# Sixteen weight loads moved from SyncE's queue to GpSimd's

## The chip, the cores and the metric

The kernel runs on one core of one Trainium2 chip. The metric is the device time of one execution in microseconds (us). The core has five engines that run their own instruction queues side by side: TensorE (PE; its weight loads are shown as PEld), VectorE (DVE), ScalarE (ACT), GpSimd (POOL) and SyncE (SP). Transfers between main memory and the on-chip memory are carried out by 16 DMA engines. An instruction on some engine's queue issues the transfer; a semaphore tells when it has landed.

## The reference

Two blocks follow each other. The first is a gated linear recurrence over 768 tokens (S) for 4 batches (B) and 8 heads (H) with head size 48 (D), with complex gates. The second is a two-layer MLP on the 3,072 resulting rows of 384 numbers, with a leaky rectifier that has one slope per feature:

```python
mag = np.sqrt(a_re * a_re + a_im * a_im)
scale = np.minimum(mag, 0.999) / (mag + 1e-06)
a_re_n, a_im_n = (a_re * scale, a_im * scale)
for t in range(S):
    new_re = ar * S_re - ai * S_im          # ar, ai: the gates of token t
    new_im = ar * S_im + ai * S_re
    S_re, S_im = (new_re + kv, new_im)      # kv: outer product of k[t] and v[t]
    y[:, :, t] = np.einsum('bhd,bhde->bhe', q[:, :, t], S_re)

x = y.transpose(0, 2, 1, 3).reshape(B * S, H * D)   # 3072 x 384
h = x @ w_in                                         # w_in: 384 x 2048
g = np.maximum(h, 0.0) + alpha * np.minimum(h, 0.0)
return (g @ w_out).astype(np.float32)                # w_out: 2048 x 384
```

The two weight matrices arrive as 64-bit floating point numbers. The kernel loads them as raw 32-bit words and makes 32-bit floats of them on the chip.

## The kernel before, in words

The 3,072 tokens are cut into 24 units of 128 tokens, six for each batch, and each unit holds all eight heads. The recurrence is not stepped through token by token. Inside a unit it is solved by doubling over block lengths 1, 2, 4, 8, 16 and 32 (the tile KQ is multiplied on DVE by decays T at line 638, and PE forms products at line 597), and a state St is carried from one half unit to the next.

**Gates.** The function `gates` turns a_re and a_im of 1, 2 or 3 units at a time into decays and phases. It loads both into the tile gate (line 264). For the last units of a batch a memset on GpSimd (line 263) clears the last column first. DVE begins with line 272, which needs a_re; line 284 is the first that needs a_im. The phases are stored to main memory as phs (line 325), the decays as decs (line 362), after a small memset on GpSimd (line 352). Each unit reads its part back as PP (line 508) and T (two loads, line 515). DVE's first work on a unit (line 580) needs PP, its first doubling step (line 638, reading WQ and T) needs T.

**Other loads of a unit.** KQ takes four loads (lines 500 and 502). In the last unit of a batch GpSimd clears the tail of KQ (line 495). V takes three small loads, VL takes ten of 24 or 48 KB (line 548) and two from a scratch copy of v called vsc (line 552; vsc is written at line 481). The result of a unit goes out as ysc (line 779) and comes back, turned, as xT (lines 795 and 800), the input of the MLP.

**Weights.** The function `pieces` loads both matrices raw, in eight parts each, in the order in0, out0, in1, out1 ... in7, out7. Each part is 768 KB: 128 partitions with three rows of 2,048 bytes for w_in or two of 3,072 for w_out. There are four regions, used in turn, so a load has to wait until ACT has read the part that was loaded four before it. The function `to_f32` turns a part into 32-bit floats in five instructions: three on ACT, which read the raw words (lines 436, 438, 440; after the last one the region is free), and two on DVE (lines 444 and 446). Only then can PE use the weights, at lines 820, 842, 870 and 960.

**Masks.** At the start GpSimd builds four masks out of memsets, affine selects (lines 173 and 175) and copies (line 183). DVE uses them at line 621.

**The order.** Nothing reorders the instructions while the kernel runs. Each function above is a task that stops at every `yield`. A string of letters written out by hand (`ORDER`, lines 30 to 70) says which task goes on next, each letter running one task up to its next `yield`. So the string fixes the order of instructions in each engine's queue. An engine executes its queue strictly in order, and an instruction that waits holds back all behind it. Before the change every load and store of the kernel is issued by SP, in one hardware queue. GpSimd has only the masks and some memsets.

Of the kernel before, what the change touches and what calls it, by code (L numbers as in the profile page):

```python
# [98 lines left out]
def kernel(  # L99
# [32 lines left out]
    nc = tc.nc  # L132
# [248 lines left out]
    def region(name, f):  # L381
        i = (2 * f + (name == "out")) % 4
        at = 18 * MT + i * 4 * DM
        return R[f"raw{i}"], shared[:, at:at + 4 * DM]
# [8 lines left out]
    def pieces():  # L393

        t = yield DMA(8)
        with nc.allow_non_contiguous_dma(reason="one token"):
            nc.sync.dma_start(start[0:D2:2], kv_in[:, :, :, 0].rearrange("b d h -> d b h"))
        done["start", 0] = t
        t = yield DMA(8)
        nc.sync.dma_start(al_1, alpha)  # L400
        t = yield DVE(NF, t)
        nc.vector.tensor_scalar(out=al_1, in0=al_1, scalar1=-1.0, scalar2=1.0, op0=ALU.mult, op1=ALU.add)
        done["alpha", 0] = t

        if words:
            wi = w_in.bitcast(U32).rearrange("(c p) (f e two) -> f p c e two", p=P, e=2 * P, two=2)
            wo = w_out.bitcast(U32).rearrange("(f r p) (e two) -> f p r e two", p=P, r=2, two=2)
        else:
            wi = w_in.rearrange("(c p) (f e) -> f p c e", p=P, e=2 * P)
            wo = w_out.rearrange("(f r p) e -> f p r e", p=P, r=2)  # L410
        for f in range(NF // 2):
            for name, src in (("in", wi), ("out", wo)):
                t = yield DMA(788 if words else 394, takes=(region(name, f)[0],))
                raw = region(name, f)[1]
                if words:
                    raw = raw.bitcast(U32).rearrange("p (c e two) -> p c e two", c=src[f].shape[1], two=2)
                else:
                    raw = raw[:, 0:NK * 2 * P].rearrange("p (c e) -> p c e", c=src[f].shape[1])
                raws[name, f] = raw
                nc.sync.dma_start(raw, src[f])  # L420
                done["raw", name, f] = t

    def to_f32(dst, *key):
# [671 lines left out]
    with tc.manual_schedule():  # L1095
        for i, g in enumerate(GATES):
            plan.add(gates(i, *g))
        plan.add(loads())
        plan.add(half_rows())
        plan.add(loads_v())  # L1100
        plan.add(pieces())
        plan.add(weights("in"))
        plan.add(weights("out"))
        for u in range(NU):
            plan.add(unit(u))
        plan.add(loads_x())
        plan.add(all_mlp())
        plan.run(ORDER)
# [37 lines left out]
```

## Time and profile before

| | |
|---|---|
| median of 3 runs | 773.71 us (771.02 to 776.0) |
| profiled execution | 772.89 us |
| its span in the profile | 771.2 us, 26,837 instructions |
| PE busy | 680.0 us (88%) |
| DVE busy | 606.4 us (79%) |
| ACT busy | 491.8 us (64%) |
| POOL busy | 12.3 us (2%), 48 instructions |
| DMA | 130.61 MB, mean 169 GB/s; hardware queue q1 128.91 MB |
| the sixteen weight loads (line 420) on SP | 8 with a median of 607 ns, 8 with 462 ns; from 8.3 to 155.5 us |

The profile divides the span into 40 equal slices and gives each engine's busy share of a slice in tenths, 9 being 90% or more. The row DMA is the mean busy share of the 16 DMA engines. A timeline line gives the start in us, the duration in us, the engine, the line of the kernel, the operation, the tile written and the tile read, shapes and the count. A bracket at its end tells how long the engine sat idle before it, and what ended the idle time. SPq is SP's queue of transfer issues: the duration is that of the issue, not of the transfer. A windows line gives, for a stretch of the span, the busy us of PE, PEld, DVE, ACT and POOL with instruction counts, then the granted TensorE clock, the DMA share (which can pass 1 where packets overlap) and GB/s.

### The profile page before, as it was taken

To read this page: it belongs to the slowest core of one execution; us is meant where nothing else is said; L and a number is where in the kernel's file an instruction comes from. 1 tells how busy PE (TensorE), PEld (TensorE's weight loads), DVE (VectorE), ACT (ScalarE), POOL (GpSimd) and SP (SyncE) were. 2 spreads that over 40 slices of the span, in tenths; PEclk is the share of its full clock that TensorE was granted. 3 is DMA by queue.
4 is the path that set the end of the run, shared out by engine and by line. 5 is a ranking of instruction groups with operands and counts; after the bars stand their busy time and mean duration, and the time that the engine had idled before them with its cause. 6 is when DMAs were issued, how large, how long until landed. Compare 5 with 4: busy or idle time off the path is not lost.

```text
span 771.2 us, 26837 instructions
## 1 busy us (share of the span) xinstructions
PE 680.0 (88%) x11728; PEld 585.2 (76%) x11728; DVE 606.4 (79%) x798; ACT 491.8 (64%) x933; POOL 12.3 (2%) x48
## 2 busy tenths in 40 slices
PE   0024687899999999999999999999999999999998
PEld 0013565667776888888888888888988888889987
DVE  7888879999999699898998699889977747652323
ACT  7967787896557667857775756856676454453330
POOL 5000000000000000000000000000000000000000
PEclk9999578999999999999999999999999999999999
DMA  9979899679677687686568745794556535411000
GB/s 246 274 216 262 241 286 267 179 228 281 147 168 193 189 199 198 185 236 143 148 164 225 192 99 141 203 277 96 153 141 191 135 88 122 124 38 58 1 21 20
DMA packets 177180, 130.61 MB, mean 169 GB/s; under 512 B 66280, under 2 KB 168424, under 8 KB 176616
## 3 DMA queue, kind: packets, MB, share of 16 engines
q1 hardware_dynamic: 177064, 128.91, 63.1%
q8 instruction: 92, 1.51, 0.8%
q14 instruction: 24, 0.20, 0.1%
HBM read 100.52 MB, written 35.42 MB: 176 GB/s over the span
## 4 chain that ended last, share of the span: by engine, by line
PE 55%; DVE 12%; DMA 8%; ACT 7%; SPq 6%; issue 3%; DVEq 0%; ACTq 0%
PE ps_h L842 17%; PE ps_o L960 15%; PE ps_h L820 4%; PE ps_lv L597 4%; DVE KQ L638 4%; PE ps_y L761 4%; PE ps_o L870 3%; DMA T<-decs 3%; PE ps_kv L721 3%; PE ps_y L747 3%; SPq L548 2%; DMA PP<-phs 2%; PE ps_kt L709 1%; PE ps_h L960 1%; DVE WQ L580 1%
## 5 line engine op out<-in xcount | busy, mean ns | idle before, releaser
L842 PE MATMUL ps_h<-xT,w_in_sb 128*128 128x256 f32 x960 | 228.6, 384 | 0.4 <-DVE shared L857 0.2
L842 PEld LDWEIGHTS ps_h<-xT,w_in_sb 128*128 128x128 f32 x960 | 176.5, 190 | 22.9 <-DVE shared L857 0.9
L638 DVE TENSOR_TENSOR KQ<-KQ,T 96x1024 f32<-96x1024 f32 x120 | 145.8, 1216 | 24.2 <-PE ps_lv L597 12.1
L857 DVE TENSOR_TENSOR shared<-shared,ps_h 128x512 f32<-128x512 f32 x80 | 54.5, 682 | 76.8 <-ACT shared L855 76.7
L960 PE MATMUL ps_o<-w_out_sb,shared 128*128 128x192 f32 x624 | 111.9, 329 | 2.5 <-ACT top L976 1.4
L960 PEld LDWEIGHTS ps_o<-w_out_sb,shared 128*128 128x128 f32 x624 | 102.2, 190 | 5.8 <-ACT top L976 2.1
L851 ACT ACTIVATE shared<-ps_h 128x512 f32<-128x512 f32 x80 | 47.7, 597 | 82.2 <-PE ps_h L842 81.7
L661 ACT COPY WQ<-KQ 96x1024 f32<-96x1024 f32 x48 | 50.0, 1041 | 52.2 <-DVE KQ L638 52.1
L960 PE MATMUL ps_o<-shared 128*128 128x192 f32 x448 | 81.0, 330 | 0.7 <-DVE top L966 0.7
L855 ACT ACTIVATE shared<-shared,al 128x256 f32<-128x256 f32 x160 | 74.7, 504 | 2.0
L960 PEld LDWEIGHTS ps_o<-shared 128*128 128x128 f32 x448 | 73.0, 190 | 3.3 <-DVE top L966 1.1
L820 PE MATMUL ps_h<-xT,w_in_sb 128*128 128x256 f32 (+1 forms) x240 | 55.2, 359 | 11.8 <-DMA xT<-ysc 11.8
L597 PE MATMUL ps_lv<-WQ 96*32 96x32 f32 x2304 | 34.9, 204 | 33.9 <-DVE WQ L580 27.0
L597 PEld LDWEIGHTS ps_lv<-WQ 96*32 96x32 f32 x2304 | 26.7, 116 | 48.6 <-DVE WQ L580 27.0
L820 PEld LDWEIGHTS ps_h<-xT,w_in_sb 128*128 128x128 f32 x240 | 43.3, 204 | 25.1 <-DMA xT<-ysc 11.9
L870 PE MATMUL ps_o<-w_out_sb,shared 128*128 128x384 f32 x128 | 52.8, 522 | 3.5 <-DVE shared L829 2.6
L774 ACT COPY T<-ps_y 48x256 f32<-48x256 f32 x96 | 31.5, 365 | 33.1 <-PE ps_y L761 32.4
L677 ACT COPY W<-KQ 96x512 f32<-96x512 f32 x48 | 30.7, 640 | 28.3 <-DVE KQ L638 28.0
L761 PE MATMUL ps_y<-A,VL 64*48 64x64 f32 x2304 | 45.1, 224 | 2.5 <-DMA VL<-vsc 2.5
L611 ACT ACTIVATE A<-ps_lv,columns 128x64 f32<-128x64 f32 x144 | 38.7, 329 | 9.5 <-PE ps_lv L597 9.5
L761 PEld LDWEIGHTS ps_y<-A,VL 64*48 64x48 f32 x2304 | 37.5, 123 | 7.7 <-DMA VL<-vsc 2.9
L597 PE MATMUL ps_lv<-KQ,W 96*32 96x32 f32 x1536 | 24.0, 204 | 14.6 <-ACT W L677 12.1
(106 smaller groups left out, 963.2 us busy)
## 6 DMA issues: line engine op xcount, KB each, us to landing
T<-decs SPq DMA_DIRECT2D x48, 384.0 KB
PP<-phs SPq DMA_DIRECT2D x24, 387.0 KB
KQ<-in_q_dram SPq DMA_DIRECT2D x48, 192.0 KB
phs<-gate SPq DMA_DIRECT2D x14, 577.5 KB
decs<-gate SPq DMA_DIRECT2D x7, 1152.0 KB
KQ<-in_k_dram SPq DMA_DIRECT2D x40, 192.0 KB
vsc<-in_v_dram SPq DMA_DIRECT2D x24, 288.0 KB
VL<-vsc SPq DMA_DIRECT2D x48, 144.0 KB
```

Source lines behind the costliest of these rows:

```text
L597: nc.tensor.matmul(t[64 * i + j:64 * i + j + HC // 2, p], lhsT=keys(n, g), rhs=queries(n, g), start=True, stop=True)
L611: nc.scalar.activation(a[:, :, cols], t[:, :, at:at + name], AF.Copy, scale=s)
L638: nc.vector.tensor_tensor(out=x, in0=x if x0 is None else x0, in1=m, op=ALU.mult)
L661: nc.scalar.copy(z.rearrange("p i n t -> p i (n t)").rearrange("p i (m h) -> p m i h", h=h), bass.AP(tensor=KQ.tensor, offset=KQ.offset + ...
L761: nc.tensor.matmul(o, lhsT=Vp[h][64 * i:64 * i + 64, s, e_ * D:(e_ + 1) * D], rhs=a, start=False, stop=(s == 1 and h == LEVELS[-1]))
L820: nc.tensor.matmul(p, lhsT=w_in_sb[:, f // 2, kk, f % 2 * P:(f % 2 + 1) * P], rhs=x_of[m][:, kk, c * P:(c + n) * P], start=(kk == 0), stop ...
L842: nc.tensor.matmul(p[:, i], lhsT=w_in_sb[:, f // 2, kk, i * P:(i + 1) * P], rhs=x_of[m][:, kk], start=(kk == 0), stop=(kk == NK - 1))
L851: nc.scalar.activation(gt, p, AF.Relu, scale=-1.0)
L855: nc.scalar.activation(some_, some_, AF.Copy, scale=al_1[:, f + i:f + i + 1])
L857: nc.vector.tensor_tensor(out=gt, in0=gt, in1=p, op=ALU.add)
L870: nc.tensor.matmul(sums[0], lhsT=gt, rhs=w_out_sb[:, f], start=(f == start), stop=(f == stop))
L960: nc.tensor.matmul(z, lhsT=a[:, i], rhs=w[:, i], start=i == 0, stop=i == F2 - 1)
```

## The change

The sixteen loads of raw weights are issued by GpSimd in place of SP. The letters of `ORDER`, the regions, the waits on regions, and every other instruction stay. The loads thus leave the hardware queue that SP feeds and go into a queue of GpSimd's, and on GpSimd they stand among its masks and memsets, where `ORDER` has them.

```diff
@@ -417,7 +417,7 @@
                 else:
                     raw = raw[:, 0:NK * 2 * P].rearrange("p (c e) -> p c e", c=src[f].shape[1])
                 raws[name, f] = raw
-                nc.sync.dma_start(raw, src[f])
+                nc.gpsimd.dma_start(raw, src[f])
                 done["raw", name, f] = t
```

GpSimd's queue, with the loads in place: affine select, **in0**, affine select, **out0**, two copies (end of the first mask), gate memset (line 352), **in1**, mask memset, **out1**, the rest of the second, the third and the fourth mask, gate memset (352), two gate memsets (263), **in2, out2, in3, out3**, gate memset (352), **in4, out4, in5, out5, in6, out6**, KQ memset (495), **in7, out7**, gate memset (352), and then the memsets of the later batches.

## The prediction

> **What bounds the kernel now.** I read the page's slices first, to see in which stage the sixteen loads lie.
>
> ```profile
> PE   0024687899999999999999999999999999999998
> DVE  7888879999999699898998699889977747652323
> DMA  9979899679677687686568745794556535411000
> ```
>
> One slice is 19.3 us. From slice 8 on (154 us) PE is full to the end, so the end comes as late as PE's work is handed over before that. In slices 0 to 7 PE waits, DVE is 80 to 90% busy and the DMA engines are full. All sixteen loads are issued between 8.3 and 155.5 us, in that first stage. What counts there is DVE: its program is one fixed queue, and of the first 160 us it sits idle 24. So I went through DVE's timeline for idle time (last bracket) that a transfer ended, and then through SP's for what stood ahead of that transfer.
>
> ```profile
> 46.76 0.76 DVE L272 TENSOR_SCALAR gate<-gate 128x1152 f32<-128x1152 f32 x1 [2.06 <-DMA gate<-in_a_re_dram]
> 49.82 1.22 DVE L638 TENSOR_TENSOR KQ<-WQ,T 96x1024 f32<-96x1024 f32 x1
> 80.03 1.22 DVE L580 TENSOR_TENSOR WQ<-KQ,PP 96x1024 f32<-96x1024 f32 x1 [4.45 <-DMA PP<-phs]
> 112.77 0.76 DVE L272 TENSOR_SCALAR gate<-gate 128x1152 f32<-128x1152 f32 x1 [2.87 <-DMA gate<-in_a_re_dram]
> 115.08 1.22 DVE L638 TENSOR_TENSOR KQ<-WQ,T 96x1024 f32<-96x1024 f32 x1 [0.83 <-DMA T<-decs]
> ```
>
> ```profile
> 39.33 0.37 SPq L264 DMA_DIRECT2D gate<-in_a_re_dram  x1
> 39.75 1.23 SPq L515 DMA_DIRECT2D T<-decs  x2
> 41.08 1.22 SPq L264 DMA_DIRECT2D gate<-in_a_im_dram  x1
> 57.71 0.43 SPq L420 DMA_DIRECT2D shared<-in_w_in_dram  x1
> 60.78 0.55 SPq L420 DMA_DIRECT2D shared<-in_w_out_dram  x1
> 61.38 0.47 SPq L420 DMA_DIRECT2D shared<-in_w_in_dram  x1
> 70.74 0.40 SPq L420 DMA_DIRECT2D shared<-in_w_out_dram  x1
> 71.25 0.40 SPq L508 DMA_DIRECT2D PP<-phs  x1
> ```
>
> I call the loads in0, out0, in1 ... out7. All share one hardware queue, so PP at 71.25 stands behind four weight loads. The trace's single packets (2,048 bytes for w_in, 3,072 for w_out) put in2, out2, in3 and out3 at 58.8 to 77.1 us. PP lands only 8.76 us after its issue, and DVE loses 4.45. The stretches of 3 us show how full the engines are (last two columns: DMA share, GB/s).
>
> ```profile
> 42.00:45.00 3.00, 0.66 (x32) 0.52 (x32) 2.70 (x4) 1.88 (x2) 0.00 (x0) 1.00 1.09 283
> 45.00:48.00 3.00, 0.00 (x0) 0.00 (x0) 1.24 (x2) 0.45 (x1) 0.00 (x0) 1.00 1.15 295
> 51.00:54.00 3.00, 0.66 (x32) 0.52 (x32) 2.86 (x4) 3.00 (x8) 0.00 (x0) 1.00 0.48 164
> 54.00:57.00 3.00, 1.01 (x5) 0.75 (x6) 3.00 (x3) 2.98 (x8) 0.00 (x0) 1.00 0.11 27
> 75.00:78.00 3.00, 0.00 (x0) 0.00 (x0) 0.58 (x2) 3.00 (x4) 0.00 (x0) 0.50 1.24 219
> ```
>
> **What moves.** GpSimd's queue is nearly empty, so a load's new time is that of the GpSimd instruction ahead of it in the written order, or of the last ACT read of its region (L440).
>
> ```profile
> 1.52 1.14 POOL L173 TENSOR_SCALAR_AFFINE_SELECT mask<-mask 128x128 f32<-128x128 f32 x1
> 12.75 0.10 POOL L352 MEMSET gate<- 128x6 f32 x1 [1.09 <-DVE gate L316]
> 39.66 0.14 POOL L263 MEMSET gate<- 128x3 f32 x2 [13.77 <-DMA KQ<-in_k_dram]
> ```
>
> in0 stands behind the L173 that ends at 2.7 (was 8.26), and out0 behind one more affine select, at about 5 (8.92). in1 and out1 follow the memset of 12.75 (15.57, 26.80). in2, out2 and in3 follow the L263 memset of 39.66, with regions free at 25.6, 37.2 and 36.3 (57.71, 60.78, 61.38). out3 is free at 54.3 (70.74), and in4 follows the memset of 73.45 (88.80). The others go 5 to 28 us earlier. In short, loads leave the places where SP reached them and go where the gates' memsets release them.
>
> **The issue itself.** SP loses 16 instructions, 8 by 607 and 8 by 462 ns (medians of line 420): 8.6 us. Two of them are in the chain that ended last (0.40 at 70.74, 1.07 at 103.20); the others mostly precede waits. Beyond those two I take -1 us, bounds -3 to 0. GpSimd gains 16 issues. The trace has none there: from below SP's 0.46, from above GpSimd's longest instruction, 1.14. I take 1.1, its own engine's row, so 18 us on an engine busy 12.3 of 771. What queues behind: the last three masks now come after the memset of 12.75, so 12.75 + 2.2 + their 7.2 = 22 us, and L621 first reads one at 36.26. The KQ memset of 122.38 waits for out6 (region free 109.1), the gate memset of 153.23 for out7 (127.6). All are covered by 14 us or more, and so is the data: the smallest lead of a new issue over ACT's L436 is 14 us (in5: 95.1 against 109.32).
>
> **The sharing.** No two busy queues run side by side in this trace. From below, the second queue takes nothing from the first; from above, all of its bytes go first. I take equal halves, nearest to what engines already at 1.09 to 1.15 can give.
>
> Start: in0 and out0 (packets 11.2 to 16.4, so 5.2 us of the engines) now run from about 4.4. a_im of the second gate block (last packet 10.7) has 6.3 us of queue work left then; in halves both loads pass before it ends. It is 5.2 later, landing near 17.7 with the 1.8 us between last packet and reader that a_re shows at 46.76. DVE wants it at 14.52 (L284): +3.2, bounds 0 to 5.2. DVE and ACT are full from there to 30 us, so nothing gives it back.
>
> At 40 us: in2, out2 and in3 (about 3.3 each, as in0: 10 us) start with a_re, T and a_im. a_re's last packet at 44.9 moves by 3.9, T's at 48.3 by 7.3. DVE's L638 at 49.82 needs T, which it found just landed: +7.3, bounds 0 to 10. [...]
>
> At 80 us: no weights before PP but out3, so the 4.45 goes: -4.45. DVE is late by then, so T or ACT is next. At 112: in5 leaves its place ahead of a_re and T (packets 104.9 to 108.4), but in6 and out6 arrive at 108 to 109: -1.5, bounds -3.7 (2.87 + 0.83) to 0.
>
> Sum: 3.2 + 7.3 - 4.45 - 1.5 - 1 = **+3.6 us**. The profiled execution took 772.9 (span 771.2, 1.7 around it): 776.4. The median of the runs shown is 0.8 above it, so **777**.
>
> **Rivals.**
> - *Spare room, faster.* The second queue fills 51 to 60 us, where SP trickles out 24 KB loads and the engines stand at 0.11 to 0.48, and takes nothing at 40. Then -4.45 - 3.7 - 1 = -9: 765. For it: those idle 6 us. Against it: 1.09 to 1.15 just when the loads are released. 0.12.
> - *Weights first, slower.* From the point where the new queue gets over half, in2, out2 and in3 hold a_re and T for all 10 us, and in0 with out0 take 5.2. VL for unit 0 is late too, so SP stands longer at the ysc store ahead of PP (L779), and of the 4.45 nothing returns: +15, 789. [...] 0.25.
> - *Nothing of note.* The loads land 14 us ahead and DVE is the bound; losses and gains cancel: 773. The change would then do what it says with no effect. 0.15.
> - *Starved descriptors.* GpSimd's copies (L183) take 0.51 for two at 3.9 us, with DVE mostly idle, and 0.88 at 10.8, with DVE full. If building a transfer stops whenever DVE runs, a load released at 40 finds no gap from 48 to 69, and ACT's L436 of in2 (63.16) waits until then: +8, 781 to 785. Against it: a factor of 1.7 on 1.1 us is small beside 14 us of lead. 0.05. [...]
>
> **How the numbers follow.** My forecast, 774 to 781, has 0.43. The range takes in the spare-room case in part and weights-first to its end: 766 to 789. A measurement here tells about 1%, 7.7 us, from no change. Faster than 766: 0.09. Slower than 781.4: 0.25, 0.05 and a tail of 0.03, so 0.33. Within: 0.58.
>
> **What would show it.** DVE should have new idle time before L284 near 15 us and before L272 or L638 near 50, ended by gate or T loads, and no PP wait at L580 near 80 to 85. In the queue table a second queue should hold 12.6 MB, with its 2,048-byte packets from about 4 us. I am wrong if DVE's wait at L272 near 47 stays at 2 us (no sharing loss), if ACT waits at L436 for weights (starved), or if GpSimd's memsets end any wait.

## The result and the profile after

| | before | after |
|---|---|---|
| median, us | 773.9 (771.02 to 776.0, 4 runs) | 784.0 (782.01 to 785.86, 4 runs) |
| ratio, 95% interval | 1 | 1.0133 (1.0089 to 1.0176) |
| span of the profiled execution, us | 771.2 | 783.3 |
| PE busy, us | 680.0 | 679.2 |
| POOL busy, us | 12.3 (48 instructions) | 28.8 (64) |

The kernel became slower by 1.3%: 10.3 us, of which the forecast of 777 had 3.6. PE does the same work; it gets it later. The TensorE clock does not explain that: over the first 160 us the granted clock was 0.95 after and 0.87 before. Nor did the DMA engines get more to do: the packets took 63.1% of a span of 771.2 us before, and 57.5% and 5.0% of one of 783.3 after. Ratios and intervals below are of undisturbed executions alone, while the profiled one of the middle group with a pause (span 783.6) was disturbed, and is read for where waits stand and not for its total.

First the page of after: engines in 40 slices (19.6 us each, tenths), then two lines of the queue table (packets, MB, share of 16 engines).

```profile
PE   0015486689999999999999999999999999999998
DVE  6869886999999889988998699889977657652323
DMA  8895999839866796696568645894657526412000
...
q1 hardware_dynamic: 171688, 116.32, 57.5%
q0 software_dynamic: 2816, 12.58, 5.0%
```

The reader is to see that PE is full from slice 9 on, one later than before, and that the loss lies ahead of it: slices 2 to 8 read 1, 5, 4, 8, 6, 6, 8, where before they read 2, 4, 6, 8, 7, 8, 9. The weights are 12.58 MB in a queue q0 of their own, as forecast. They come in 2,816 packets where SP's queue, in 177,064 - 171,688, needed 5,376. That is half as many, so a packet of the new queue is about twice as long. This becomes important below.

Next, the timeline of DVE after: start, duration, engine, line, operation, and in the last bracket the idle time before it and what ended it. Places that the prediction named stand beside others that it did not.

```profile
9.32 0.56 DVE L284 SCALAR_TENSOR_TENSOR gate<-gate 128x384 f32<-128x384 f32 x1 [2.40 <-DMA gate<-in_a_im_dram]
29.59 1.22 DVE L580 TENSOR_TENSOR WQ<-KQ,PP 96x1024 f32<-96x1024 f32 x1 [1.64 <-DMA PP<-phs]
48.98 0.76 DVE L272 TENSOR_SCALAR gate<-gate 128x1152 f32<-128x1152 f32 x1 [2.07 <-issue]
56.39 1.22 DVE L638 TENSOR_TENSOR KQ<-WQ,T 96x1024 f32<-96x1024 f32 x1 [4.38 <-DMA T<-decs]
81.23 1.22 DVE L580 TENSOR_TENSOR WQ<-KQ,PP 96x1024 f32<-96x1024 f32 x1
89.52 1.22 DVE L638 TENSOR_TENSOR KQ<-WQ,T 96x1024 f32<-96x1024 f32 x1 [2.54 <-DMA T<-decs]
116.35 0.76 DVE L272 TENSOR_SCALAR gate<-gate 128x1152 f32<-128x1152 f32 x1 [1.09 <-DMA gate<-in_a_re_dram]
125.22 1.22 DVE L638 TENSOR_TENSOR KQ<-WQ,T 96x1024 f32<-96x1024 f32 x1 [7.38 <-DMA VL<-in_v_dram]
```

The last line is labelled VL, but this instruction reads only WQ and T. Of T's 768 packets of 1,024 bytes the last ended at 124.59, just ahead of DVE's start at 125.22, so this too is a wait for T.

The same instructions of before and after, side by side, give how late DVE is at each point:

| DVE instruction (start before) | after | later by |
|---|---|---|
| L284, first gate block (7.24) | 9.32 | 2.1 |
| L580, first unit (25.76) | 29.59 | 3.8 |
| L272 (46.76) | 48.98 | 2.2 |
| L638 with T (49.82) | 56.39 | 6.6 |
| L638 with T (84.96) | 89.52 | 4.6 |
| L272 (112.77) | 116.35 | 3.6 |
| L638 with T (115.08) | 125.22 | 10.1 |

Three large steps up and one down: +2 to +4 at the start, +4.4 at 50 us, -2.0 by 90 us where the wait for PP is gone (line 580 at 81.23 has no bracket), and **+6.6 at 115 us**, which was not forecast. Smaller ones lead back a little between them. By 265 us DVE is 7.9 late, and the span ends 12.1 later. On the way PE has two waits that the trace of before does not have (line 709 for ACT's T 1.2, line 842 for St 1.4). Whether these belong to the change no run settles; medians of the kernel before differ by over 2 us.

POOL's timeline of after shows that the issues go where the prediction put them.

```profile
2.62 0.87 POOL L420 DMA_DIRECT2D shared<-in_w_in_dram  x1
5.02 0.89 POOL L420 DMA_DIRECT2D shared<-in_w_out_dram  x1
...
42.87 0.77 POOL L420 DMA_DIRECT2D shared<-in_w_in_dram  x1
43.63 0.72 POOL L420 DMA_DIRECT2D shared<-in_w_out_dram  x1
44.35 0.77 POOL L420 DMA_DIRECT2D shared<-in_w_in_dram  x1
61.06 0.72 POOL L420 DMA_DIRECT2D shared<-in_w_out_dram  x1 [15.93 <-ACT w_out_sb L440]
...
113.43 0.76 POOL L420 DMA_DIRECT2D shared<-in_w_in_dram  x1 [10.01 <-ACT w_in_sb L440]
114.73 0.72 POOL L420 DMA_DIRECT2D shared<-in_w_out_dram  x1 [0.55 <-DMA VL<-in_v_dram]
```

Three bursts matter: in0 and out0 at 2.6 to 5.0, three loads at 42.9 to 44.4, and in6 and out6 at 113.4 and 114.7. The later two come 3 to 5 us after their forecast times, as DVE is late by then. One issue takes 0.72 to 1.02 us, also at 42.87, where DVE is busy 2.78 of 3 us.

How the two queues shared the 16 DMA engines, counted from the trace's packet records (4-byte ones left out):

```
                     GpSimd's queue             SP's queue
after, 47 to 55 us   472 packets, 79% of time   465 packets, 21%
packet, median       4,096 bytes 175 ns         1,024 bytes 46 ns
                     6,144 bytes 253 ns         384 to 1,536 bytes 22 to 66 ns
```

In this stretch they went packet for packet (472 to 465), and the longer packets took four fifths of the time (79%).

### The profile page after: what moved, and what is told of

It is laid out like the page before. It is cut to its first block, busy times and chain, and to the rows that moved or that the text cites. A ratio compares the mean times of both kernels' runs of the same rounds, so it can differ in the third digit from the quotient of the medians.

```text
span 783.3 us, 26845 instructions
## 1 busy us (share of the span) xinstructions
PE 679.2 (87%) x11728; PEld 584.4 (75%) x11728; DVE 606.9 (77%) x798; ACT 492.3 (63%) x933; POOL 28.8 (4%) x64
## 3 DMA queue, kind: packets, MB, share of 16 engines
q1 hardware_dynamic: 171688, 116.32, 57.5%
q0 software_dynamic: 2816, 12.58, 5.0%
## 5 line engine op out<-in xcount | busy, mean ns | idle before, releaser
L638 DVE TENSOR_TENSOR KQ<-KQ,T 96x1024 f32<-96x1024 f32 x120 | 145.8, 1216 | 23.0 <-PE ps_lv L597 12.0
L597 PEld LDWEIGHTS ps_lv<-WQ 96*32 96x32 f32 x2304 | 26.7, 116 | 53.1 <-DVE WQ L580 30.9
L638 DVE TENSOR_TENSOR KQ<-WQ,T 96x1024 f32<-96x1024 f32 x24 | 29.2, 1217 | 19.4 <-DMA T<-decs 12.0
```

The lines of the kernel that those rows point to most:

```text
L597: nc.tensor.matmul(t[64 * i + j:64 * i + j + HC // 2, p], lhsT=keys(n, g), rhs=queries(n, g), start=True, stop=True)
L638: nc.vector.tensor_tensor(out=x, in0=x if x0 is None else x0, in1=m, op=ALU.mult)
```

## The experiments

**Theory A (bytes).** The loss is the DMA time that weights take, at their new places, from the loads SP issued at about the same time; each burst has its own price. **Theory B (the issue).** GpSimd's issuing itself costs: its time, its queue order, or a slowing beside a busy DVE. The expectations name more. For the runs up to the tiny loads, theory C says that the start makes all of the loss and the rest is its echo. For the runs with cut loads, C says that GpSimd's queue is served first whatever its packets are. Theory D says that any second queue costs the same. In kernels with added lines, line numbers are shifted by 1 to 3.

### One burst at a time

Three kernels move one group each; together the groups make up the change.

```diff
-                nc.sync.dma_start(raw, src[f])
+                (nc.gpsimd if f < 2 else nc.sync).dma_start(raw, src[f])         # e1_start
+                (nc.gpsimd if f in (2, 3) else nc.sync).dma_start(raw, src[f])   # e2_mid
+                (nc.gpsimd if f > 3 else nc.sync).dma_start(raw, src[f])         # e3_late
```

> Only in0, out0, in1 and out1 go through GpSimd; the other twelve stay with SP. Theory A (the new queue's bytes crowd out what SP sends at the same time, so each place of release costs for itself): the start's part alone. DVE is late by 2 us at L284 of the first gate block (9.3 against 7.2) and by about 2 at L272 near 47 to 49, no more than 1 us of wait for T at L638 near 52, the PP wait near 82 stays at about 4.5; time +1 to +3 over before. Theory B (GpSimd's own work beside DVE costs, so much per load): 4 of 16 loads, +2.5, without new waits on transfers. Theory C (all of the loss comes from the start, the rest is its echo): about +10.

> Only in2, out2, in3 and out3 go through GpSimd. Theory A: no loss until 47, then DVE waits 4 to 7 us for T at L638 near 50, and the PP wait near 80 (4.45) shrinks to under 1; net 0 to +3 us. Theory B: +2.5 without new waits on transfers. Theory C: 0.

> Only in4 to out7, eight loads, go through GpSimd. Theory A: nothing before 80; the PP wait near 80 stays; in6 and out6, released at about 108, stop the T that is issued at 107, so that DVE waits 5 to 8 us at L638 near 115 to 122; +4 to +8 us. Theory B: +5 spread over 70 to 160 us. Theory C: 0.

| | median, us | ratio to before (95%) |
|---|---|---|
| in0 to out1 | 777.62 | 1.0043 (1.0009 to 1.0078) |
| in2 to out3 | 773.5 | 0.9991 (0.996 to 1.0023) |
| in4 to out7 | 780.97 | 1.0083 (1.0052 to 1.0114) |

The three add up to +1.17%, against +1.33% for the whole. DVE's timelines, the start group first:

```profile
9.21 0.56 DVE L284 SCALAR_TENSOR_TENSOR gate<-gate 128x384 f32<-128x384 f32 x1 [2.19 <-DMA gate<-in_a_im_dram]
29.29 1.22 DVE L580 TENSOR_TENSOR WQ<-KQ,PP 96x1024 f32<-96x1024 f32 x1 [1.46 <-DMA PP<-phs]
```

The middle group:

```profile
45.98 0.76 DVE L272 TENSOR_SCALAR gate<-gate 128x1152 f32<-128x1152 f32 x1 [1.26 <-DMA gate<-in_a_re_dram]
53.37 1.22 DVE L638 TENSOR_TENSOR KQ<-WQ,T 96x1024 f32<-96x1024 f32 x1 [4.36 <-DMA T<-decs]
78.04 1.22 DVE L580 TENSOR_TENSOR WQ<-KQ,PP 96x1024 f32<-96x1024 f32 x1
```

The late group:

```profile
79.06 1.22 DVE L580 TENSOR_TENSOR WQ<-KQ,PP 96x1024 f32<-96x1024 f32 x1 [5.14 <-DMA PP<-phs]
88.29 0.35 DVE L829 SCALAR_TENSOR_TENSOR shared<-shared,al,ps_h 128x128 f32<-128x128 f32 x1 [4.95 <-ACT shared L827]
122.14 1.22 DVE L638 TENSOR_TENSOR KQ<-WQ,T 96x1024 f32<-96x1024 f32 x1 [5.16 <-DMA T<-decs]
```

The changed kernel's waits at line 284, for T near 50 and for T near 122 each appear with their own group and with no other. In the middle group the new wait of 4.36 for T and the lost wait of 4.45 for PP (line 580 at 78.04 has no bracket) cancel. The late group makes most of the loss. The start alone makes a third of it, so the first theory C is out.

### Which of the late loads

```diff
-                nc.sync.dma_start(raw, src[f])
+                (nc.gpsimd if f > 5 else nc.sync).dma_start(raw, src[f])
```

> Only in6, out6, in7 and out7 are issued by GpSimd (released by their regions near 109 us and later); in4 to out5 stay with SP. The eight loads from in4 on together gave 1.0083, with new waits for PP (5.14 near 79), for ACT at line 829 (4.95 near 88) and for T (5.16 near 122). Theory A: the wait for T near 114 to 122 is from in6 and out6 that now stand beside T and VL, and comes back alone: +3 to +6 us, 1.004 to 1.008, while the waits near 80 and 88 are those of before (4.45 for PP, none above 1.5 at 829). Rival: the wait near 122 followed from the earlier ones, in4 to out5 alone make the loss: 0.999 to 1.002 and no wait for T above 1.5.

Measured: 782.53 us, 1.0083 (1.0052 to 1.0115), the whole loss of the late group with half of its loads. From DVE's timeline, then POOL's, then SP's (SPq: issue of a transfer), and last SP's line for the same T in the kernel before:

```profile
120.79 1.22 DVE L638 TENSOR_TENSOR KQ<-WQ,T 96x1024 f32<-96x1024 f32 x1 [8.00 <-DMA T<-decs]
```

```profile
107.13 0.88 POOL L420 DMA_DIRECT2D shared<-in_w_in_dram  x1 [33.06 <-DMA shared<-in_w_in_dram]
108.44 0.72 POOL L420 DMA_DIRECT2D shared<-in_w_out_dram  x1 [0.43 <-DMA VL<-in_v_dram]
```

```profile
107.27 1.78 SPq L515 DMA_DIRECT2D T<-decs  x2
```

```profile
107.05 1.27 SPq L515 DMA_DIRECT2D T<-decs  x2
```

The issues of T began at 107.27, those of in6 and out6 at 107.13 and 108.44, and T reached DVE at 120.8, 13.5 us after its issue began. In the kernel before T was issued from 107.05 on, and DVE had it by 115.08, 8.0 us later. The packet records show what lies between. Before, T's 768 packets ran from 109.47 to 114.59 us, and in6 and out6 were issued on SP only at 123.87 and 128.68. Here T's packets began as early, at 109.72, but GpSimd's began at 109.54, and T's last one ended at 119.81. In SP's queue the two loads stood behind T. From a queue of their own they did not wait for it: from 110 to 112 us the queues went packet for packet (104 to 112), and from 110 to 116 GpSimd's had 71% of the busy time. So of the late loads in6 and out6, beside T, explain the loss; the waits near 79 and 88 of the late group brought nothing on top (T was then awaited for 5.16 in place of 8.00).

A fixed price per load, wherever it is released, does not fit: four loads of the middle group cost -0.7 us (1.8 at most by the interval), the four of this run 6.4 (4.0 at least).

### The issue alone, and another queue

In the first kernel SP keeps the weights, and GpSimd issues sixteen additional loads of 8 bytes per row at the same places of its order. They do not wait for regions, so six of them leave in one burst from 72.7 to 76.7 us. In the second all sixteen are issued by ACT.

```diff
+    tiny = consts.tile([P, NF, 3, 2], U32, tag="tiny")
...
                 nc.sync.dma_start(raw, src[f])
+                some = tiny[:, 2 * f + (name == "out"), 0:src[f].shape[1]]
+                nc.gpsimd.dma_start(some, src[f][:, :, 0])                 # e4_tiny
```

```diff
-                nc.sync.dma_start(raw, src[f])
+                nc.scalar.dma_start(raw, src[f])                           # e5_act
```

> All sixteen loads stay with SP; beside each, GpSimd issues a load of 8 bytes of every row of the same weights into a small tile that nothing reads: the same sixteen issues with as many rows at GpSimd's places (without the waits on regions), and the masks moved as in the change, but next to no bytes. Theory A: within 2 us of before. Theory B: +8 to +10, most of the loss. Theory C: +2.

> All sixteen loads are issued by ACT, in a second hardware queue, in place of GpSimd's; on ACT they stand among its own work. Theory A (packets take turns, and the GpSimd queue's are of 4,096 and 6,144 bytes where SP's are of 384 to 1,536): ACT's queue sends single rows of 2,048 and 3,072 bytes, so beside it SP's packets get 35 to 45% of the engines where they got 10 to 25% beside GpSimd's; waits for a_im, T and PP shrink by a third or more. Loads come due later too, since ACT is busy where GpSimd is idle, but ACT pays 16 issues of about 0.5 us. +2 to +8. Theory D (any second queue costs the same, whatever its packets): shares as in the change and +10.

The tiny loads: 776.74 us, 1.002 (0.999 to 1.005). The issues take 0.72 to 1.03 us as in the change, and the queue moves 0.04 MB. At most 0.5 of the change's 1.33% can lie with them, so theory B falls as the main cause. What remains is the order in which bytes move: in the change, packets of the two queues ran side by side from 47 to 55 us (472 to 465). A gain from SP's sixteen issues was not seen apart.

ACT's queue: 799.74 us, 1.0286 (1.0242 to 1.0329). It did not answer by its time what it was made for, whether a second queue costs the same whatever its packets are. ACT reaches the issues only when its own work lets it, and then waits for the very loads. From its timeline:

```profile
63.20 0.38 ACTq L420 DMA_DIRECT2D shared<-in_w_in_dram  x1
68.33 0.91 ACT L436 ACTIVATE top<-shared 128x768 f32<-128x768 f32 x1 [2.83 <-DMA shared<-in_w_in_dram]
...
80.20 0.38 ACTq L420 DMA_DIRECT2D shared<-in_w_out_dram  x1
...
86.89 0.89 ACT L436 ACTIVATE top<-shared 128x768 f32<-128x768 f32 x1 [5.40 <-DMA shared<-in_w_out_dram]
```

One load issued at 63.20 is awaited from 65.5 on, another one issued at 80.20 from 81.5 on, and DVE then stands 15.93 at line 316 for ACT, whose copy at line 774 had waited 8.60 for PE as well. What the run does show is a size: ACT's queue moved the weights in packets of 2,048 and 3,072 bytes, 84 and 121 ns, like SP's. Packets of double length (4,096 and 6,144 bytes) were seen in GpSimd's queue alone. Where both queues had work, from 21 to 23 us, they too went packet for packet (302 of ACT's, almost all of 2,048 bytes, to 305 of SP's of 512 and 516), and ACT's longer ones took 75% of the time.

### Later releases

If the bursts collide with SP's loads, let them come later. Memsets on GpSimd (0.27 us each, of a small unused tile) stand ahead of the first load of a burst: 14 before in0, 40 before in2 and 36 before in6 with all loads on GpSimd; 36 before in6 with the late group; 40 before in2 with the middle group.

```diff
+    pause = consts.tile([P, 112], F32, tag="pause")
...
-                nc.sync.dma_start(raw, src[f])
+                for _ in range({("in", 0): 14, ("in", 2): 40, ("in", 6): 36}.get((name, f), 0)):   # e6_paced
+                    nc.gpsimd.memset(pause, 0.0)
+                nc.gpsimd.dma_start(raw, src[f])
```

> The change, with small memsets on GpSimd (112 numbers a row, a scratch tile) ahead of three loads, so that it issues them later: 14 ahead of in0 (after most of the masks, near 12 us), 40 ahead of in2 (near 52, after T) and 36 ahead of in6 (near 122, after T). Queue, packets and issues are those of the change; only the times of release differ. Theory A: the waits at L284, at L638 near 56 and at L638 near 125 go; 8 to 12 us come back of the change's 10, so between -3 and +3 against before. Theory B or D (the queue itself costs): still +8 to +11.

> As the late group by itself (in4 to out7 through GpSimd), with 36 memsets ahead of in6 alone. Theory A: DVE's wait for T near 122 (5.2 us in the run without the memsets) falls under 2, the loss near 80 (in4 and out4 beside PP and xT) stays; +3 to +5 where it was +6.4. Theory D: +6 to +7.

> As the middle group by itself (in2, out2, in3, out3 through GpSimd), with 40 memsets ahead of in2, so that the three loads go out near 50 us, where the engines stand idle beside SP's small VL loads, and not at 40 beside a_re and T. Theory A: the wait for T near 53 (4.4) goes, the PP wait near 78 stays away: -2 to -5 against before. Against it: VL of unit 0 and ysc come later and hold PP; then 0.

| | median, us | ratio to before (95%) |
|---|---|---|
| all, with pauses | 788.64 | 1.0151 (1.0102 to 1.02) |
| late group, in6 with a pause | 783.21 | 1.0088 (1.0058 to 1.0118) |
| middle group, in2 with a pause | 779.21 | 1.0013 (0.9977 to 1.0049) |

No pause gained anything. Theory A had forecast -3 to +3, +3 to +5 and -5 to -2 us. Measured were +11.7 (7.9 to 15.5), +6.8 (4.5 to 9.2) and +1.0 (-1.8 to 3.8), so the times miss all three forecasts, and the first two are about what the rivals B and D had. What keeps A is that the waits moved with the releases, and that four loads cost little at one place and much at another. The middle group is the clearest: in2 is issued at 50.30, T no longer waits, PP does not either, and still there is no gain: at line 580 near 80 DVE is 2.4 us earlier than before, hardly more than the 2.0 without the pause. DVE's timeline of this kernel, then PE's:

```profile
74.11 1.36 DVE L316 SCALAR_TENSOR_TENSOR gate<-gate 128x1152 f32<-128x1152 int16 x1 [5.03 <-ACT gate L313]
```

```profile
67.79 2.89 PE L764 MATMUL ps_y<-A,VL 64*48 64x64 f32 x80 [5.24 <-DMA VL<-vsc]
```

PE waits 5.24 for VL (2.29 in the kernel before), ACT's copy of the product waits 6.0 for PE (2.24 before), its line 313 stands behind that copy, and DVE waits 5.03 for line 313. VL's packets are of 384 bytes. From 53 to 62 us GpSimd's queue had 593 packets and 91% of the busy time, SP's 540. I had taken the stretch from 50 us on for free since the engines stood at 0.11 to 0.48 there. They do, but the loads that trickle out in it are small ones with a reader close behind. In the kernel with all pauses the waits that had been named went or shrank (line 284, T near 50, T near 117 to 1.72), and others came: PP at 30.24 (3.93), line 316 at 77.11 (3.95), line 829 at 134.57 (4.72). With the late group's pause, in6 goes out at 107.44, 1.2 after T's first issue, and the wait for T is 2.79; PE then waits 2.28 at 123 for VL and DVE 3.45 at line 829. I can't exclude that some other release would gain; these three show that a later one in the same stretch meets the next load.

### The two loads in the chain

Only out3 and in5, the two that stood in the chain that ended last, go to GpSimd.

```diff
-                nc.sync.dma_start(raw, src[f])
+                (nc.gpsimd if (name, f) in (("out", 3), ("in", 5)) else nc.sync).dma_start(raw, src[f])
```

> Only out3 and in5 are issued by GpSimd, the two weight loads that stand in the chain that ended last before; the other fourteen stay with SP. Theory A (bytes): what a moved load costs or gains is the DMA time that it takes from others at its new place. out3 goes to 54.3 us, when its region is free and the engines stand at 0.11 to 0.48; its 3.3 us then lie in front of PP's 71.25 no longer, so of the wait for PP (4.45) 3 to 4 go. in5 goes from 103.2 to about 97, between engines at 1.05 and 1.11 both times: -1 to +1. So -5 to -2 us, a ratio of 0.993 to 0.998. What speaks against it is the run with four loads delayed to 50 us, where VL came late and turned the gain into another wait; by that, if VL (from 49.9 us) is delayed by out3, PE's line 764 waits 1 to 3 us and the ratio is 0.998 to 1.003. Theory B (the issue on GpSimd costs): two issues, nothing to see, 1.000.

Measured: 775.83 us, 0.9992 (0.997 to 1.0014). PP's wait is gone here too, and smaller ones take its place. DVE's timeline, then PE's:

```profile
72.57 1.36 DVE L316 SCALAR_TENSOR_TENSOR gate<-gate 128x1152 f32<-128x1152 int16 x1 [3.01 <-ACT gate L313]
```

```profile
65.42 0.44 PE L761 MATMUL ps_y<-A,VL 64*48 64x64 f32 x2 [2.90 <-DMA VL<-vsc]
```

The gain of 2 to 5 us did not come. PE's wait for VL, 2.90, is in the stated 1 to 3, but was 2.29 before; with the 0.89 right behind it (0.16 before) it grew by 1.3, as line 316's did. DVE's 4.45 went in parts: line 316 waits 3.01 (1.67 before), line 580 2.43 near 103, and line 638 2.56 for T near 114 (0.83 before). Up to 175 us DVE is busy for 150.6 us, as before, so its idle time there has not shrunk. No version that I ran is faster than the kernel before by more than its interval.

### Does the packet's length decide?

All sixteen loads by GpSimd, cut into single rows (40 issues), or into quarters of the columns (64 issues).

```diff
-                nc.sync.dma_start(raw, src[f])
+                for k in range(src[f].shape[1]):                                                    # e10_rows
+                    nc.gpsimd.dma_start(raw[:, k], src[f][:, k])
...
+                w = raw.shape[2] // 4                                                               # e12_quarters
+                for k in range(4):
+                    nc.gpsimd.dma_start(raw[:, :, k * w:(k + 1) * w], src[f][:, :, k * w:(k + 1) * w])
```

> All sixteen weights by GpSimd, but each in two or three loads of one row, so 40 issues in place of 16, at the same places in the order. Theory A with turns by packet: in the change GpSimd's packets were two rows long (4,096 and 6,144 bytes, 175 and 253 ns) and took 0.70 to 0.97 of the engines while both queues were busy. Single rows (2,048 and 3,072 bytes, some 84 and 122 ns) against SP's 46 to 72 ns would take 0.55 to 0.7. The waits at lines 284, 638 (T near 56) and 638 near 125 then shrink by a fifth to a third: ratio 1.007 to 1.012. Theory C (the queue is served first whatever its packets are): share still 0.7 to 0.97, waits and time as in the change, 1.012 to 1.016. Theory B (issues cost): 24 issues more of 0.7 to 1.0 us each, every wait for weights or on GpSimd longer: above 1.016.

> All sixteen weights by GpSimd, each in four loads of a quarter of the columns (512 and 768 bytes at a time), so 64 issues, at the same places in the order. Splitting by rows (40 issues) left GpSimd's packets at 4,096 and 6,144 bytes, its share at 0.72 to 0.93 from 46 to 53 us, and the wait for T near 55 at 4.43 (4.38 in the change); it is the control for the issues spread in time. Theory A with turns by packet: packets of 512 to 1,536 bytes take about as long as SP's (46 to 72 ns), so GpSimd's share while both queues are busy falls to 0.4 to 0.6, T overtakes half of the weights, and the wait near 55 falls from 4.4 to between 1 and 3; the time between the run by rows and half of its loss, 1.003 to 1.007, but up to 1.010 if the shorter packets take a quarter longer in all. Theory C (GpSimd's queue is served first, whatever its packets): share 0.7 or more, the wait near 55 4 or more, 1.007 to 1.013. Theory B (issues cost): the waits at GpSimd's releases grow, weights come late at line 436, above 1.013.

By rows: 781.46 us, 1.0066 (1.0045 to 1.0087). By quarters: 784.99 us, 1.0119 (1.0071 to 1.0167). Neither gave the packets that were wanted. With rows they stayed at 4,096 and 6,144 bytes, although each load now has only 2,048 or 3,072 bytes per partition, and the share from 46 to 53 us at 81%. With quarters they were 3,072 to 4,608 bytes. So this queue joined short runs here. The sizes seen fit two runs of 2,048 (4,096), two of 3,072 (6,144), eight of 512 (4,096), and six of 768 (4,608) with four as a rest (3,072). Cutting the loads did not make its packets short. Part of the gain by rows is at the start: with in0 spread over three issues from 2.62 to 5.69, DVE's line 284 has no wait. T near 55 is awaited for 4.43, as in the change.

The quarters have a result of their own. Their share from 47 to 55 us fell to 59% (331 packets to 698), probably because four issues of 0.76 us release a load more slowly. DVE still waited as long for T:

```profile
56.07 1.22 DVE L640 TENSOR_TENSOR KQ<-WQ,T 96x1024 f32<-96x1024 f32 x1 [4.42 <-DMA T<-decs]
```

Of T's 768 packets 90% had ended at 50.7 us, against 53.1 in the change, but the last at 55.2 against 55.6. DVE waits for the last one. Why the last packets remained is open: the records do not tell which of the 16 engines a packet ran on. By its time and its wait for T this run lies where theory C (served first) had put it, and by the share alone where A had. What speaks against C is the equal numbers of packets in the change (472 to 465): a queue that is served first would leave the other fewer. So theory A holds for the place of release and for loads no longer waiting behind T; that shorter packets would give a smaller loss was not shown.

## Why the prediction was right and wrong

The range (766 to 789) holds the time. The likeliest time (777, own range 774 to 781) does not: the sum of +3.6 is too small by 6.7, and one term makes about all of that. That the range held owes much to its width: its upper end came from a rival (weights first) whose prices were not met.

| term | forecast, us | measured |
|---|---|---|
| start, a_im at L284 | +3.2 | DVE 2.1 later; the group alone +3.3 (0.7 to 6.0) |
| 40 us, T behind three loads | +7.3 | wait of 4.38; DVE +4.4 |
| 80 us, the wait for PP goes | -4.45 | goes; T next (2.54), DVE -2.0 |
| both of these, middle group | +2.85 | the group alone -0.7 (-3.1 to +1.8) |
| **112 us** | **-1.5 (-3.7 to 0)** | **L272 waits 1.8 less, T 6.6 more: DVE +4.8; in6 to out7 alone +6.4 (4.0 to 8.9)** |
| SP's sixteen issues | -1 | not seen apart |

(A group's us are its ratio and interval less 1, times the 773.8 or 776.1 of before.) The size of the start's term was partly luck: it was reckoned for the second gate block, and the waits came at the first one (2.40) and for PP (1.64).

**The step that failed** is the one at 112 us: "in5 leaves its place ahead of a_re and T (...), but in6 and out6 arrive at 108 to 109: -1.5, bounds -3.7 (...) to 0." It let the arrival of in6 and out6 diminish a gain and never become a loss; zero was its upper bound without a reason. At 40 us the same working, three loads released beside a_re and T, had been given +7.3. Here two loads stood beside the next a_re and T, and DVE waited 7.38 for it. The gain itself came, at line 272 (2.87 before, 1.09 after); the loss at T was put at nothing. I counted weights that left SP's queue ahead of T, and took those issued after T for harmless, as they were in SP's queue (in6 issued at 123.87, T's last packet at 114.59). From another queue they were not: T's packets, which ran for 5.1 us before (109.47 to 114.59), ran for 10.9 after (113.67 to 124.59).

**The sharing** was the second miss: equal halves were taken, 79% was measured from 47 to 55 us, the side of the rival "weights first". The price of that rival did not come with it. It has +10 at 40 us and nothing back at 80; measured were +4.4 and -2.0. One reason is the start: the first of the three loads was issued at 42.87 and its packets are seen from 46.4, whereas I had them start together with a_re. By 46.4 a_re's packets were nearly through, and its wait stayed at 2.07 (2.06 before), so the 3.9 forecast for a_re did not occur. What the 79% go with is the length of GpSimd's packets: 4,096 and 6,144 bytes (175 and 253 ns), twice those of the weights in SP's queue, beside 1,024 (46 ns) of SP's.

**The other rivals.** Spare room: the engines had some from 51 to 57 us (DMA share 0.29 before), but VL's small loads needed their turn then (middle group with pause). Nothing of note: excluded by the interval. Starved descriptors: its 781 to 785 contains the time, but not its mechanism; the issues took 0.72 to 1.02 us beside a busy DVE, ACT never waits at line 436 for weights in the changed kernel, and sixteen issues without the bytes cost 0.2% (-0.1 to 0.5).

**The signs.** New idle time at line 284 came, but at the first gate block (9.32), not at the second near 15. It came at line 638 near 50, the PP wait was gone, and the second queue has 12.58 MB with packets from 4.7 us, in twice the 2,048 bytes. No wait of DVE up to 200 us is put down to GpSimd's memsets. "I am wrong if DVE's wait at L272 near 47 stays at 2 us" was a bad sign to choose: it stayed at 2.07, and the sharing loss came at T.

## What to carry to other kernels

A load moved to another engine's queue no longer stood behind what was issued before it: it ran beside that and could finish first (in the changed kernel T was issued from 112.20 on and in6 at 113.43; in6's last packet ended at 121.27, T's at 124.59). So a price has to be set at every place where it is released, against all that is outstanding there (T's packets took 10.9 us in place of 5.1 here), not just against what was issued later. With the DMA engines full (share 1.00 to 1.12 from 78 to 90 us in the changed kernel), taking bytes away from one wait (PP, 4.45) gave them to the next (T, 2.54 in the changed kernel; VL, 2.90 in the run with two loads), and delaying them did the same. A stretch of low DMA share (0.48 and 0.11 from 51 to 57 us before) was not free room, as the small loads in it had a reader right behind (PE then waited 5.24 for VL).

## What the runs showed of the hardware

- GpSimd's queue moved the same rows in packets of 4,096 and 6,144 bytes (175 and 253 ns), where SP's and ACT's queues used 2,048 and 3,072 (84 and 121 to 122 ns). Cutting the loads into rows of 2,048 bytes left the packets as they were; cutting them into runs of 512 and 768 bytes gave 4,096 and 4,608 with rests of 3,072. A packet of 4,096 bytes made of eight runs took 218 ns, one of two runs 175.
- Over stretches of some us two queues shared the engines packet for packet (472 to 465; 593 to 540; 302 to 305 with ACT's), so GpSimd's with its 4 to 6 KB packets got 79% of the time beside packets of about 1 KB, and 91% beside 384-byte ones. In other stretches they did not (196 to 769 from 112 to 118 us in the run with in6 to out7); whether GpSimd's queue was empty on some engines by then the records do not tell.
- From GpSimd's issue to the first packet 2.1 us passed at 2.62 and 3.5 at 42.87; the issue itself took 0.72 to 1.02.
